# An attention backward kernel on Trainium2: where the fp32 transposes of the result tile stand, and which blocks of the exponentials TensorE transposes beside them

## The chip, the cores and the metric

One core of a Trainium2 chip. The metric is the device time of one execution in microseconds; lower is better. Before: 2212.41 us, the median of three runs (2210.66 to 2218.44). A step of the loop below takes about 1.6 us, so most times in this text are in nanoseconds.

## The reference

The kernel computes a transformer block and all its gradients in one launch: x of 2048 x 512, 32 heads of 16, an MLP of width 1792. Cut to what matters:

```python
def _A_ref(x, wqkv, wo):                       # attention
    qkv = (x @ wqkv).reshape(B, S, 3, H, Dh).transpose(2, 0, 3, 1, 4)
    q, k, v = qkv[0], qkv[1], qkv[2]
    scores = jnp.einsum("bhqd,bhkd->bhqk", q, k) * (Dh ** -0.5)
    p = softmax(scores, axis=-1)
    o = jnp.einsum("bhqk,bhkd->bhqd", p, v)
    return o.transpose(0, 2, 1, 3).reshape(B, S, D) @ wo
...
x = A_x
xn = _layernorm(x)
s = _A_ref(xn, A_wqkv, A_wo)
g = _silu(_B_ref(xn, B_w1, B_b1, B_w2, B_b2))  # the MLP
return x + s * g
...
_out, _vjp = jax.vjp(_f, A_x, A_wqkv, A_wo, B_w1, B_b1, B_w2, B_b2)
_grads = _vjp(grad_out)
```

The change lies in the attention part alone, where the forward pass and the backward pass of q, k and v are done together.

## The kernel before

`attention_core` works through 64 *blocks*: 16 pairs of heads, times four chunks of 512 queries. A block has 16 *steps*, one for each 128 keys, so there are 1024 steps, counted by `g`; `g % 16` is the place in the block. Per step and for both heads of the pair these quantities are made, with the names that the profile uses:

- `s` (L1093): scores of 128 keys by 512 queries for each head, two matmuls into one PSUM tile of two banks; there is one such tile.
- `ets` (L1102): ScalarE's exp of `s`, 128 x 1024, written into a ring in SBUF that holds 12 steps. This is E, in eight blocks of 128 keys by 128 queries (two heads, four query blocks).
- `d` (L1115): dO times V, two matmuls, each into a PSUM bank of its own out of a pool of three (`ps_d`).
- `gts` (L1132): VectorE's product of `d` and `ets`, two multiplies of 128 x 512.
- `tT` (L1177): seven of the eight blocks of E, transposed by TensorE into one PSUM tile (`ps_t`, one buffer); the eighth goes through a DMA (`ekd`). ScalarE and VectorE copy `tT` into the SBUF tiles `ek` (both L1189): `VCOPY` says for each place in the block how many of the seven VectorE takes, ScalarE takes the rest. Where VectorE takes some, ScalarE's copy waits for VectorE's.
- `X` (L1207, L1210, L1214): sums over the 16 steps of a block, in one PSUM bank, 128 x 512 fp32: the numerators of o and dq, the row sums, and others, all with queries along the free dimension.
- `Z` (L1291): dK and dV of an earlier block, from the transposed E (`ek`) and the DMA-transposed `gts` (`gk`), weighted by `W`; four matmuls a step, 20 steps behind. VectorE adds Z to `acc` (L1303, L1305) at places 3 and 11.

The order on each engine is the order of the code (no scheduler moves anything). The loop for step `g` emits:

```python
emit_d(g, 0); emit_s(g + 1, 0); emit_s(g + 1, 1); emit_d(g, 1)
emit_exp(g + 1)
emit_T(g - 1)
emit_XT(g)
emit_x(g - 1, "e"); emit_x(g - 1, "l"); emit_x(g - 1, "g")
emit_z(g + ZOFF)
emit_mult(g)
emit_xs(g - 1)
emit_fin(g)
...
emit_acc(g + ZOFF)
...
emit_cT(g - 1, 0, 7 - VCOPY[(g - 1) % 16], nc.scalar.copy)
emit_dmat(g)
```

So TensorE runs d, s, s, d, the transposes of the step before, (XT), X, Z. ScalarE runs the exp of the next step and then the copy of the last step's `tT`. VectorE runs the first multiply, its share of the `tT` copy (inside `emit_mult`), the second multiply, and at some places one copy or addition more.

After the last step of a block, VectorE copies X to SBUF (`xs`, L1223, at place 0 of the next block). At place 2 (`FIN_AT`) TensorE transposes `xs` in four fp32 pieces of 128 x 128 (`XT`, L1233) into a tile that takes a turn in the pool of `d`; VectorE copies it (`xt`, L1245, 512 columns) and takes the reciprocal of the row sums (`rL`, L1255); GpSimd makes from it the weights `W` that Z needs from place 4 on, and the parts of o and dq (L1256 to L1271). Four GpSimd lines of these need the second half of XT (XG) only.

The DMA transposes of `gts` and of the eighth block of E (L1148, L1158, L1162, L1164) stand in SyncE's queue and read the ring of E and `gts`.

Of the kernel before, what the change touches and what calls it, by code (L numbers as in the profile page):

```python
# [8 lines left out]
bf16 = mybir.dt.bfloat16  # L9
f32 = mybir.dt.float32  # L10
ACT = mybir.ActivationFunctionType
ALU = mybir.AluOpType
# [1016 lines left out]
def attention_core(ctx, ctx_r, tc, k, grads, Oall, dQall, dKVT_out, ident_f32, ident_bf, npairs=16, nqc=4):  # L1029
    nc = tc.nc  # L1030
# [3 lines left out]
    ps_t = ctx.enter_context(tc.tile_pool(name="ps_t", bufs=1, space=PSUM, reuse_waits="tile"))  # L1034
    ps_d = ctx.enter_context(tc.tile_pool(name="ps_d", bufs=3, space=PSUM, reuse_waits="tile"))
# [8 lines left out]
    xsp = sb("xsp", 1)  # L1044
    finp = sb("finp", 1)
# [19 lines left out]
    NB = len(blocks)  # L1065
    NSTEP = NB * 16
    st_s, st_d, st_et, st_gt, st_T = {}, {}, {}, {}, {}
    blk = [dict(Gk={}, Ek={}) for _ in range(NB)]
    cur = {}

    def a_unit(g):
        return (g // 16, g % 16) if 0 <= g < NSTEP else None
# [43 lines left out]
                         start=True, stop=True, tile_position=(r, 0))  # L1116


    VCOPY = (0, 0, 0, 0, 1, 1, 1, 2, 1, 2, 0, 0, 1, 1, 1, 0)

    def emit_mult(g):
        a = a_unit(g)
        if a is None:
            emit_cT(g - 1, 7 - VCOPY[(g - 1) % 16], 7, nc.vector.tensor_copy)
            return
        kb = a[1]
        if kb % 2 == 0:
            cur["gts"] = gtp.tile([128, 2, 2, 512], bf16, name="gts")
        gts = cur["gts"]
        st_gt[g] = gts  # L1130
        for hj in range(2):
            nc.vector.tensor_tensor(out=gts[:, kb % 2, hj, :].rearrange("k (b q) -> k b q", b=4),  # L1132
                                    in0=st_d.pop((g, hj))[:].rearrange("k (b q) -> k b q", b=4),
                                    in1=st_et[g][:, :, hj, kb % 4, :], op=ALU.mult)
            if hj == 0:
                emit_cT(g - 1, 7 - VCOPY[(g - 1) % 16], 7, nc.vector.tensor_copy)

    def emit_dmat(g):
# [12 lines left out]
        sl = g // 4 % 3  # L1151
        if kb % 8 == 4:
            ek = ekd.tile([128, 2, 4, 128], bf16, name="ekd")
            blk[j]["Ek"][(kc - 1, 3)] = ek[:, 0]
            blk[j]["Ek"][(kc, 3)] = ek[:, 1]
            blk[j]["ekd"] = ek
            if sl == 0:
                nc.sync.dma_start_transpose(out=ek[:, 0], in_=ets[:, 2, 3, 1].rearrange("k a q -> k (a q)"))  # L1158
        if kb % 8 == 6:
            ek = blk[j].pop("ekd")  # L1160
            if sl == 0:
                nc.sync.dma_start_transpose(out=ek[:, 1], in_=ets[:, sl, 0, 0].rearrange("k a q -> k (a q)"))  # L1162
            else:
                nc.sync.dma_start_transpose(out=ek[:].rearrange("q c a k -> q (c a) k"),  # L1164
                                            in_=ets[:].rearrange("k s b h a q -> k (s b h) (a q)")[:, 8 * sl - 1:8 * sl + 1]
                                            .rearrange("k x q -> k (x q)"))

    def emit_T(g):
        a = a_unit(g)
        if a is None:  # L1170
            return
        kk = a[1] % 4
        et = st_et[g]
        t = ps_t.tile([128, 7, 128], bf16, name="tT")
        for i in range(7):
            b = i + a[1] // 4 % 2
            nc.tensor.transpose(t[:, i, :], et[:, b // 2, b % 2, kk, :], ident_bf[:])  # L1177
        st_T[g] = t
        if kk == 0:
            cur["ek"] = ekc.tile([128, 4, 7, 128], bf16, name="ek")  # L1180
            blk[a[0]]["Ek"][a[1] // 4] = cur["ek"]

    def emit_cT(g, lo, hi, copy):

        a = a_unit(g)
        if a is None or lo == hi:
            return
        j, kb = a
        copy(out=blk[j]["Ek"][kb // 4][:, kb % 4, lo:hi].rearrange("q i k -> q (i k)").bitcast(f32),  # L1189
             in_=st_T[g][:, lo:hi].rearrange("q i k -> q (i k)").bitcast(f32))  # L1190

    def emit_x(g, part):
        a = a_unit(g)
# [23 lines left out]
    def emit_xs(g):  # L1217
# [5 lines left out]
        nc.vector.tensor_copy(out=xs[:], in_=blk[j].pop("X")[:])  # L1223
        blk[j]["xs"] = xs

    def emit_XT(g):
        j = g // 16 - 1
        if g % 16 != FIN_AT or not 0 <= j < NB:
            return
        xs = blk[j].pop("xs")  # L1230
        XT = ps_d.tile([128, 4, 128], f32, name="XT", tag="d")
        for qb in range(4):
            nc.tensor.transpose(XT[:, qb, :], xs[:, qb * 128:(qb + 1) * 128], ident_f32[:])  # L1233
        blk[j]["XT"] = XT

    def emit_fin(g):
        j = g // 16 - 1
        if g % 16 != FIN_AT or not 0 <= j < NB:
            return
        p, qc = blocks[j]  # L1240
        NQq = k.op0["NATQq"]
        NQd = k.op0["NATQd"]
        XT = blk[j].pop("XT")
# [10 lines left out]
        rL = finp.tile([128, 4, 2, 1], f32, name="rL")  # L1254
        nc.vector.reciprocal(out=rL[:], in_=XG[:, :, :, 17:18])  # L1255
        nc.gpsimd.tensor_tensor(out=W2[:, :, :, 16:32], in0=nqs, in1=bc(rL[:]), op=ALU.mult)  # L1256
        ndl = finp.tile([128, 4, 2, 1], f32, name="ndl")
        nc.gpsimd.tensor_tensor(out=ndl[:], in0=XG[:, :, :, 0:1], in1=rL[:], op=ALU.mult)
        ndr = finp.tile([128, 4, 2, 1], f32, name="ndr")
        nc.gpsimd.tensor_tensor(out=ndr[:], in0=ndl[:], in1=rL[:], op=ALU.mult)  # L1260
        nc.gpsimd.tensor_tensor(out=W1[:, :, :, 0:16], in0=ndo, in1=bc(rL[:]), op=ALU.mult)
        nc.gpsimd.tensor_tensor(out=W1[:, :, :, 16:32], in0=nqs, in1=bc(ndr[:]), op=ALU.mult)
# [8 lines left out]
        nc.gpsimd.tensor_tensor(out=dQv, in0=t1[:], in1=bc(rL4[:]), op=ALU.mult)  # L1271

    def emit_z(g):
        u = z_unit(g)
# [39 lines left out]
    FIN_AT = 2  # L1314
# [5 lines left out]
    for g in range(NSTEP - ZOFF):  # L1320
        cur["g"] = g
        a = a_unit(g)
        if a is not None:
            j, kb = a
# [12 lines left out]
        emit_d(g, 1)  # L1337
# [3 lines that stand above are left out]
        emit_x(g - 1, "e")  # L1341
        emit_x(g - 1, "l")
        emit_x(g - 1, "g")
# [4 lines that stand above are left out]
        for it in [x for x in late if x[0] <= g]:  # L1348
            late.remove(it)
# [127 lines left out]
```

## Time and profile before

The profiled execution took 2212.67 us, of which 2210.8 us are the span from its first to its last instruction. The attention loop fills the span from 221.7 to 1867.4 us.

| What | Instructions | Busy, us | Mean of one, ns |
|---|---|---|---|
| multiply `gts`, VectorE L1132 | 2048 | 1361.6 | 683 |
| exp `ets`, ScalarE L1102 | 1024 | 1047.7 | 1023 |
| transposes `tT`, TensorE L1177 | 7168 | 568.1 | 219 |
| copy of `tT`, ScalarE L1189 | 1024 | 502.2 | 490 |
| matmuls `d`, TensorE L1115 | 2048 | 459.1 | 385 |
| matmuls `s`, TensorE L1093 | 2048 | 401.3 | 380 |
| copy of `tT`, VectorE L1189 | 576 | 131.6 | 229 |
| addition of Z to `acc`, VectorE L1305 | 96 | 65.5 | 682 |
| copy of XT, VectorE L1245 | 64 | 43.5 | 680 |
| fp32 transposes `XT`, TensorE L1233 | 256 | 38.9 | 274 |

Busy time is the union of the instructions' spans; since instructions of one engine overlap at their ends, the mean of one times their count is more than the busy time for matmuls that run side by side. The granted clock of TensorE was 0.997 of full speed over the whole span. The chain of waits lists the work that ended last, followed back from the end; its largest lines are `tT` (24% of the span), `d` (15%), `X` L1207 (10%), `Z` (10%).

### The profile page before, as it was taken

To read this page: it belongs to the slowest core of one execution; us is meant where nothing else is said; L and a number is where in the kernel's file an instruction comes from. 1 tells how busy PE (TensorE), PEld (TensorE's weight loads), DVE (VectorE), ACT (ScalarE), POOL (GpSimd) and SP (SyncE) were. 2 spreads that over 40 slices of the span, in tenths; PEclk is the share of its full clock that TensorE was granted. 3 is DMA by queue.
4 is the path that set the end of the run, shared out by engine and by line. 5 is a ranking of instruction groups with operands and counts; after the bars stand their busy time and mean duration, and the time that the engine had idled before them with its cause. 6 is when DMAs were issued, how large, how long until landed. Compare 5 with 4: busy or idle time off the path is not lost.

```text
span 2210.8 us, 74213 instructions
## 1 busy us (share of the span) xinstructions
PE 2154.0 (97%) x30690; PEld 1203.2 (54%) x30690; DVE 1911.7 (86%) x3638; ACT 1734.2 (78%) x2481; POOL 590.4 (27%) x1373
## 2 busy tenths in 40 slices
PE   6999999999999999999999999999999999999998
PEld 3444555555555555555555555555555555444444
DVE  6677899999999999999999999999999998797624
ACT  4664888888888888888888888888888887784214
POOL 4375213221222222221322122222222132510002
PEclk9999999999999999999999999999999999999999
DMA  7786999999999999999999999999999999999974
GB/s 232 244 277 200 200 199 192 202 198 194 204 205 195 204 196 197 201 197 202 200 196 203 199 195 198 206 194 204 197 197 206 197 210 211 300 259 235 244 200 156
DMA packets 1422066, 461.14 MB, mean 209 GB/s; under 512 B 1334622, under 2 KB 1405918, under 8 KB 1421728
## 3 DMA queue, kind: packets, MB, share of 16 engines
q1 hardware_dynamic: 1407424, 425.46, 101.4%
q0 software_dynamic: 12720, 29.37, 5.0%
q8 instruction: 240, 3.93, 0.8%
q10 hardware_dynamic: 1584, 1.57, 0.2%
q14 instruction: 98, 0.80, 0.1%
HBM read 62.79 MB, written 64.75 MB: 58 GB/s over the span
## 4 chain that ended last, share of the span: by engine, by line
PE 89%; DVE 4%; ACT 2%; issue 2%; DMA 2%; POOL 1%; SPq 1%; ACTq 0%; DVEq 0%; POOLq 0%
PE tT L1177 24%; PE d L1115 15%; PE X L1207 10%; PE Z L1291 10%; PE X L1210 5%; PE X L1214 5%; PE s L1093 3%; PE ps_dw L742 2%; PE ps_dy L912 2%; PE ps_h L352 2%; PE ps_dw L984 2%; PE ps_m L367 2%; PE ps_dh L878 2%; PE XT L1233 1%; PE ps_qkv L210 1%
## 5 line engine op out<-in xcount | busy, mean ns | idle before, releaser
L1132 DVE TENSOR_TENSOR gts<-d,ets 128x512 bf16<-128x512 f32 x2048 | 1361.6, 683 | 99.4 <-ACT ek L1189 20.5
L1102 ACT ACTIVATE ets<-s 128x1024 bf16<-128x1024 f32 x1024 | 1047.7, 1023 | 198.6 <-PE s L1093 95.5
L1177 PE MATMUL tT<-ident_bf,ets 128*128 128x128 bf16 x7168 | 568.1, 219 | 11.7 <-ACT ek L1189 1.7
L1177 PEld LDWEIGHTS <-ets 128*128 128x128 bf16 x7168 | 444.6, 97 | 237.6 <-issue 235.5
L1189 ACT COPY ek<-tT 128x448 f32<-128x448 f32 (+2 forms) x1024 | 502.2, 490 | 2.8 <-DVE ek L1189 2.1
L1115 PE MATMUL d<-QDT,KVT 32*128 32x512 bf16 x2048 | 459.1, 385 | 0.0
L1093 PE MATMUL s<-QDT,KVT 32*128 32x512 bf16 x2048 | 401.3, 380 | 3.7 <-ACT ets L1102 3.6
L1115 PEld LDWEIGHTS <-KVT 32*128 32x128 bf16 x2048 | 145.6, 91 | 323.3 <-issue 323.3
L1207 PE MATMUL X<-ets,NAT 128*32 128x256 bf16 x4096 | 300.4, 284 | 0.3 <-DVE xs L1223 0.3
L1210 PE MATMUL X<-ets,Lc 128*32 128x256 bf16 x4096 | 289.5, 273 | 0.0
L1214 PE MATMUL X<-gts,NAT 128*17 128x256 bf16 x4096 | 289.5, 273 | 0.0
L1351 POOL COPY tick<-gts 1x2 bf16<-1x2 bf16 x205 | 35.7, 174 | 612.3 <-DVE gts L1132 612.3
L1291 PE MATMUL Z<-gk,W 128*32 128x512 bf16 x2048 | 197.9, 379 | 1.0 <-DVE acc L1305 1.0
L1291 PE MATMUL Z<-ek,W 128*32 128x512 bf16 x1792 | 198.4, 379 | 0.0
L1207 PEld LDWEIGHTS <-NAT 128*32 128x32 bf16 x4096 | 106.0, 93 | 110.8 <-issue 11.3
L1256 POOL TENSOR_TENSOR W<-NATQq,rL 128x128 bf16<-128x128 bf16 x64 | 25.4, 396 | 526.1 <-DVE rL L1255 438.4
L1093 PEld LDWEIGHTS <-KVT 32*128 32x128 bf16 x2048 | 139.2, 91 | 12.8 <-issue 9.6
L1189 DVE COPY ek<-tT 128x64 f32<-128x64 f32 (+1 forms) x576 | 131.6, 229 | 0.7
L1291 PEld LDWEIGHTS <-W 128*32 128x32 bf16 x4096 | 109.8, 97 | 11.5 <-issue 1.5
L1210 PEld LDWEIGHTS <-Lc 128*32 128x32 bf16 x4096 | 107.8, 96 | 0.0
L1214 PEld LDWEIGHTS <-NAT 128*17 128x17 bf16 x4096 | 103.4, 92 | 3.0
L1291 PE MATMUL Z<-ekd,W 128*32 128x512 bf16 x256 | 97.0, 379 | 0.0
(246 smaller groups left out, 2318.7 us busy)
## 6 DMA issues: line engine op xcount, KB each, us to landing
gk<-gts SPq DMA_TRANSPOSE x512, 5.3
H1T_s<-h1r SPq DMA_DIRECT2D x28, 256.0 KB, 4.1
HGT_s<-hgT SPq DMA_DIRECT2D x8, 896.0 KB, 4.5
DH_s<-stg SPq DMA_DIRECT2D x12, 512.0 KB, 3.2
hch<-DH_s SPq DMA_DIRECT2D x12, 512.0 KB, 4.4
gp<-H1T_s SPq DMA_DIRECT2D x9, 512.0 KB, 7.6
out_dram<-ob_w POOLq DMA_DIRECT2D x36, 128.0 KB, 4.2
NAT_s<-NS SPq DMA_DIRECT2D x4, 1056.0 KB, 6.1
```

Of the source, the lines that this page charges most:

```text
L352: nc.tensor.matmul(ps[:], lhsT=w1_sb[:, ic, fc * 128:(fc + 1) * 128], rhs=yT[:, ic, g * 512:(g + 1) * 512], start=(ic == 0), stop=(ic == I ...
L367: nc.tensor.matmul(ps[:], lhsT=hgT[:, g % 2, fc, t4 * 128:(t4 + 1) * 128], rhs=w2_sb[:, fc, :], start=(fc == 0), stop=(fc == FC - 1))
L1093: nc.tensor.matmul(s[:, hj, :], lhsT=op["KVT"][r:r + 32, kb * 128:(kb + 1) * 128], rhs=op["QDT"][r:r + 32, qc * 512:(qc + 1) * 512], start ...
L1102: nc.scalar.activation(out=st_et[g][:, :, :, a[1] % 4, :].rearrange("k b h q -> k h b q"), in_=cur["s"][:].rearrange("k h (b q) -> k h b q ...
L1115: nc.tensor.matmul(d[:], lhsT=op["KVT"][r:r + 32, kb * 128:(kb + 1) * 128], rhs=op["QDT"][r:r + 32, qc * 512:(qc + 1) * 512], start=True, ...
L1132: nc.vector.tensor_tensor(out=gts[:, kb % 2, hj, :].rearrange("k (b q) -> k b q", b=4), in0=st_d.pop((g, hj))[:].rearrange("k (b q) -> k b ...
L1177: nc.tensor.transpose(t[:, i, :], et[:, b // 2, b % 2, kk, :], ident_bf[:])
L1189: copy(out=blk[j]["Ek"][kb // 4][:, kb % 4, lo:hi].rearrange("q i k -> q (i k)").bitcast(f32), in_=st_T[g][:, lo:hi].rearrange("q i k -> q ...
L1207: nc.tensor.matmul(X[r:r + 32, 0:256], lhsT=NATt[:, kb, hj, 1:33], rhs=ev, start=(kb == 0), stop=False, skip_group_check=True, tile_positi ...
L1210: nc.tensor.matmul(X[r:r + 32, 256:512], lhsT=Lc[:], rhs=ev, start=False, stop=False, skip_group_check=True, tile_position=(0, r))
L1214: nc.tensor.matmul(X[r:r + 17, 256:512], lhsT=NATt[:, kb, hj, 0:17], rhs=gv, start=False, stop=(kb == 15), skip_group_check=True, tile_pos ...
L1291: nc.tensor.matmul(Z[r:r + 32, :], lhsT=WT[j % 2][1 - part][:, qb, hj, :], rhs=mv, start=(part == 0 and qb == 0), stop=(part == 1 and qb = ...
```

## The change

XT is made in two halves, in the steps at places 2 and 3 (`fin_half`): first the half with the row sums (half 1), then the other. Each half is two fp32 transposes, written into the upper half of the PSUM tile that the same step's `tT` uses (the tile is now a full bank of 512 fp32 columns). To make room, the `tT` of places 1 and 2 leave out their first three blocks (`cut`), six in all. These six are transposed one each in the `tT` of places 4 to 9 as an eighth block (`older`), and copied by VectorE (`emit_cO`) into the `ek` tile that they belong to. VectorE copies each half of XT back over `xs` (`emit_xt`, 256 columns) between its two multiplies. GpSimd's chain is split in two accordingly: W2, ndl, ndr and W1 with half 1, Oall, t1, rL4 and dQall with the other. `VCOPY` becomes 0 at places 4 to 9, so ScalarE copies all seven blocks there, four at places 1 and 2. The first block of the loop is left as it was.

```diff
-    VCOPY = (0, 0, 0, 0, 1, 1, 1, 2, 1, 2, 0, 0, 1, 1, 1, 0)
+    VCOPY = (0, 0, 0, 0, 0, 0, 0, 0, 0, 0, 0, 0, 1, 1, 1, 0)
...
             if hj == 0:
                 emit_cT(g - 1, 7 - VCOPY[(g - 1) % 16], 7, nc.vector.tensor_copy)
+                emit_cO(g - 1)
+                emit_xt(g)
+
+    def emit_cO(g):
+        if a_unit(g) is None or not older(g):
+            return
+        kk, i = older(g)
+        nc.vector.tensor_copy(out=blk[g // 16]["Ek"][0][:, kk, i].bitcast(f32), in_=st_T[g][:, 448:512])
...
+    def cut(g):
+        return 3 if g >= 16 and g % 16 in (1, 2) else 0
+
+    def older(g):
+        n = g % 16 - 4
+        return (1 + n // 3, n % 3) if 16 <= g < NSTEP and 0 <= n < 6 else None
...
-        t = ps_t.tile([128, 7, 128], bf16, name="tT")
-        for i in range(7):
+        t = ps_t.tile([128, 512], f32, name="tT")
+        tb = t[:].bitcast(bf16).rearrange("q (i k) -> q i k", k=128)
+        for i in range(cut(g), 7):
             b = i + a[1] // 4 % 2
-            nc.tensor.transpose(t[:, i, :], et[:, b // 2, b % 2, kk, :], ident_bf[:])
+            nc.tensor.transpose(tb[:, i - cut(g), :], et[:, b // 2, b % 2, kk, :], ident_bf[:])
+        if older(g):
+            kk2, b = older(g)
+            nc.tensor.transpose(tb[:, 7, :], st_et[g // 16 * 16 + kk2][:, b // 2, b % 2, kk2, :], ident_bf[:])
...
+    def fin_half(g):
+        j = g // 16 - 1
+        if not 0 <= j < NB or g % 16 not in (FIN_AT, FIN_AT + 1):
+            return None
+        return j, (1, 0)[g % 16 - FIN_AT]
+
     def emit_XT(g):
...
-        XT = ps_d.tile([128, 4, 128], f32, name="XT", tag="d")
-        for qb in range(4):
-            nc.tensor.transpose(XT[:, qb, :], xs[:, qb * 128:(qb + 1) * 128], ident_f32[:])
-        blk[j]["XT"] = XT
+        t = st_T[g - 1] if a_unit(g - 1) is not None else ps_d.tile([128, 512], f32, name="XT", tag="d")
+        XT = t[:, 256:512].rearrange("q (b c) -> q b c", b=2)
+        for b in range(2):
+            qb = 2 * h + b
+            nc.tensor.transpose(XT[:, b, :], xs[:, qb * 128:(qb + 1) * 128], ident_f32[:])
+        blk[j]["XT"] = t[:, 256:512]
+
+    def emit_xt(g):
...
+        j, h = f
+        nc.vector.tensor_copy(out=blk[j]["xs"][:, 256 * h:256 * h + 256], in_=blk[j].pop("XT"))
...
     def emit_fin(g):
...
-        xt = xsp.tile([128, 4, 128], f32, name="xt", tag="xs")
-        nc.vector.tensor_copy(out=xt[:], in_=XT[:])
-        xf = xt[:].rearrange("q b c -> q (b c)")
+        xf = blk[j]["xs"][:]
...
+        if half == 1:
+            rL = finp.tile([128, 4, 2, 1], f32, name="rL")
+            nc.vector.reciprocal(out=rL[:], in_=XG[:, :, :, 17:18])
...
+            blk[j]["r"] = rL, ndl
+            return
+        rL, ndl = blk[j].pop("r")
...
```

More of the change, by code (lines that the diff above doesn't have):

```diff
@@ L1188, in emit_cT @@
         j, kb = a
+        c = cut(g)
+        lo = max(lo, c)
         copy(out=blk[j]["Ek"][kb // 4][:, kb % 4, lo:hi].rearrange("q i k -> q (i k)").bitcast(f32),
-             in_=st_T[g][:, lo:hi].rearrange("q i k -> q (i k)").bitcast(f32))
+             in_=st_T[g][:, (lo - c) * 64:(hi - c) * 64])
     def emit_x(g, part):
@@ L1253, in emit_fin @@
         bc = lambda ap: ap.to_broadcast([128, 4, 2, 16])
[L1254 to L1262, printed above, removed]
+        if half == 1:
+            rL = finp.tile([128, 4, 2, 1], f32, name="rL")
+            nc.vector.reciprocal(out=rL[:], in_=XG[:, :, :, 17:18])
+            nc.gpsimd.tensor_tensor(out=W2[:, :, :, 16:32], in0=nqs, in1=bc(rL[:]), op=ALU.mult)
+            ndl = finp.tile([128, 4, 2, 1], f32, name="ndl")
+            nc.gpsimd.tensor_tensor(out=ndl[:], in0=XG[:, :, :, 0:1], in1=rL[:], op=ALU.mult)
+            ndr = finp.tile([128, 4, 2, 1], f32, name="ndr")
+            nc.gpsimd.tensor_tensor(out=ndr[:], in0=ndl[:], in1=rL[:], op=ALU.mult)
+            nc.gpsimd.tensor_tensor(out=W1[:, :, :, 0:16], in0=ndo, in1=bc(rL[:]), op=ALU.mult)
+            nc.gpsimd.tensor_tensor(out=W1[:, :, :, 16:32], in0=nqs, in1=bc(ndr[:]), op=ALU.mult)
+            blk[j]["r"] = rL, ndl
+            return
+        rL, ndl = blk[j].pop("r")
         Ov = Oall[:, st0:st0 + 4, p * 32:(p + 1) * 32].rearrange("q b (h c) -> q b h c", h=2)
@@ L1271, in emit_fin @@
         nc.gpsimd.tensor_tensor(out=dQv, in0=t1[:], in1=bc(rL4[:]), op=ALU.mult)
+        blk[j].pop("xs")
     def emit_z(g):
```

16 lines of the change are left out of this document (10 added, 6 removed).

## The prediction

> **What bounds the kernel now.** I read the page first. TensorE is the chain:
>
> ```profile
> PE 2154.0 (97%) x30690; PEld 1203.2 (54%) x30690; DVE 1911.7 (86%) x3638; ACT 1734.2 (78%) x2481; POOL 590.4 (27%) x1373
> ...
> PE 89%; DVE 4%; ACT 2%; issue 2%; DMA 2%; POOL 1%; SPq 1%; ACTq 0%; DVEq 0%; POOLq 0%
> ...
> L1189 ACT COPY ek<-tT 128x448 f32<-128x448 f32 (+2 forms) x1024 | 502.2, 490 | 2.8 <-DVE ek L1189 2.1 <-PE tT L1177 0.6
> ```
>
> But matmul ends are modelled, so 97% does not say that no more fits in. For that I cut the attention stretch (221.7 to 1867.4 us, 64 blocks of 16 steps) at the starts of ScalarE's exp (L1102). Slot n runs from the exp of step n (in its block) to that of step n+1. The stretch view of one undisturbed block, slots 0 to 6:
>
> ```profile
> 659.45:661.01 1.56, 1.56 (x30) 0.90 (x29) 1.37 (x3) 1.39 (x2) 0.06 (x1) 1.00 1.29 240
> 661.01:662.57 1.56, 1.53 (x29) 0.89 (x28) 1.51 (x3) 1.45 (x2) 0.62 (x2) 1.00 1.15 258
> 662.57:664.19 1.62, 1.60 (x30) 0.97 (x30) 1.62 (x4) 1.45 (x3) 0.00 (x0) 1.00 1.33 132
> 664.19:666.17 1.98, 1.98 (x35) 1.25 (x34) 1.95 (x4) 1.45 (x3) 0.00 (x0) 1.00 1.02 228
> 666.17:667.73 1.56, 1.53 (x29) 0.88 (x27) 1.56 (x4) 1.45 (x3) 1.25 (x5) 1.00 1.25 286
> 667.73:669.33 1.60, 1.57 (x29) 0.94 (x29) 1.53 (x4) 1.45 (x2) 1.52 (x5) 1.00 0.56 127
> 669.33:670.89 1.56, 1.56 (x30) 0.90 (x29) 1.39 (x3) 1.39 (x2) 1.18 (x4) 1.00 1.28 293
> ```
>
> Columns: length, then busy time of PE, PEld, DVE, ACT, POOL, the clock, DMA. A slot is 1.56 us; only slot 3 is 1.98. The timeline says why, and what sets 1.56:
>
> ```profile
> 661.01 1.02 ACT L1102 ACTIVATE ets<-s 128x1024 bf16<-128x1024 f32 x1 [0.17 <-PE d L1115]
> 661.93 0.53 ACT L1189 COPY ek<-tT 128x448 f32<-128x448 f32 x1
> 662.03 0.38 PE L1115 MATMUL d<-QDT,KVT 32*128 32x512 bf16 x1
> 662.09 0.39 PE L1093 MATMUL s<-QDT,KVT 32*128 32x512 bf16 x2
> 662.51 0.55 PE L1177 MATMUL tT<-ident_bf,ets 128*128 128x128 bf16 x7
> ...
> 664.07 0.55 PE L1177 MATMUL tT<-ident_bf,ets 128*128 128x128 bf16 x7
> 664.46 0.61 PE L1233 MATMUL XT<-ident_f,xs 128*128 128x128 f32 x4
> 665.00 0.29 PE L1207 MATMUL X<-ets,NAT 128*32 128x256 bf16 x4
> ...
> 667.35 0.68 DVE L1305 TENSOR_TENSOR acc<-Z,acc 128x512 f32<-128x512 f32 x1
> 667.95 2.04 DVE L1132 TENSOR_TENSOR gts<-d,ets 128x512 bf16<-128x512 f32 x3
> ```
>
> From the same records, as medians over the blocks, in ns (E is the slot's exp start):
> - exp takes 1023; s, which overwrites what exp reads, starts at E+1075 or 3 after the first d, whichever is later. From s to the next exp is 487 when d went out 35 or more earlier, 520 when s comes right behind d (slots 2, 5, 13: 1613, 1600, 1601). 1075+487 = 1562 is the slot: a ring of TensorE and ScalarE, in which the first d arrives at about E+1023, some 50 early.
> - second d to first tT 362; tT to X 480 with seven transposes, 55.5 for each more or fewer; X to the next first d 660.
> - ScalarE's copy of tT (one buffer) starts at E+920 and takes 527, 473, 420 for 7, 6, 5 blocks, so 366 for 4 (estimate, 54 a block); the next tT starts 52 after it. After a copy of seven that is E+1499, 50 later than TensorE could.
> - VectorE, start to start: multiply 598, a copy of 512 columns 598, of 128 198, of 64 131, the reciprocal 121; a multiply lasts 679, and the d that reuses its buffer starts 53 after it.
> - four XT put 55+116+110+109+202 = 592 between the last tT and X, in place of 147: +445, slot 3's excess.
>
> The sixteen slots of a block without a late DMA sum to 25,523.
>
> **Part by part.** *XT out of one step, in two pairs.* Steps 2 and 3 issue four tT and two XT: 3x55.5+55+116+202 = 540 from tT to X, against 480. First d of slot 3: 1499+540+660 past the exp of slot 2 (1613 long), at 1086, so the slot is 1089+520 = 1609, not 1981: -372. Slot 4: d at 1049, s on time, 1565: +3. Slot 5: d at about 1030, 1564, -36, because ScalarE copies four blocks only in slots 3 and 4. The new wait there, tT (and ScalarE's copy, which waits too) on VectorE's copy of XT, ends at about E+1020, so ScalarE ends near 1420 and tT starts at 1470 at the latest, a few ns late. Behind acc, which slips with VectorE to 635 of slot 5, waits Z of step 4, due at 727: no loss, by 40 after the hand-over.
>
> *The copy of XT: two of 256 columns for one of 512.* No row has that width; the ends are 198 and 598 each. I take 331, since 131, 198 and 598 lie on a line of 1.04 ns a column. VectorE's work then moves: it does multiply, xt, multiply, reciprocal in step 2 (1648), and multiply, xt, multiply, acc in step 3 (2125), against slots of 1609 and 1565. Its first multiply of step 4 starts about 560 into slot 5, ends at 1240, and the second d of step 5, which takes the buffer that this multiply frees (three in turn, two a step), starts at 1295 in place of 1084. The cover that xt and acc had before is gone: slot 3's extra 372, in which VectorE caught up. Behind this d on TensorE stand step 5's transposes; with eight of them (below) the next d comes at 1295+362+536+660-1564 = 1289 of slot 6, which is then 1292+520 = 1812, not 1564: +248. Were the copies 198 wide in time there would be no late d and slot 6 would be 1656 (-156 on my sum); at 598 it would grow by 534.
>
> *The six left-out blocks, one in each of steps 4 to 9.* 55.5 each on TensorE, which the 50 of slack would nearly hide, had ScalarE's copy stayed at 384 or 320 columns. VCOPY is set to 0 there, so ScalarE copies all seven: tT starts at E+1499. 1499+536+660-1562 = 1133: s comes right behind d, and the slot is 1136+520 = 1656; from there the next tT starts at 1505, d at 1045, and that slot is 1562. So 1562 and 1656 alternate in slots 7 to 11, against 1562: +93, +94 and +10 (slot 11 was 1552). Slots 12 to 14 alternate too, seven transposes behind full copies: 1600, 1562, 1600 against 1562, 1601, 1562: +37. Slot 15 takes 1562 for 1552: +10.
>
> *VectorE's other copies*: 9 per block before, 7 of 64 and 2 of 128 columns, 9 of 64 after: -134 of work off the path in slots 6 to 14, worth nothing while TensorE waits for ScalarE. GpSimd's chain starts after the same reciprocal, some 0.4 us earlier; Z needs W two steps on. No DMA moves in its queue.
>
> Sum: -372+3-36+248+93+94+10+37+10 = +87 ns; with roundings of some 10 per slot, +75. In 63 blocks: +4.7 us. The profiled execution spans 2210.8 of 2212.67 us, and the median of the three runs is 2212.41; so span 2215.5, **2217 us**. The late-d penalty of 33 (520 less 487) is taken from rows; the Trainium skill ("TensorE: Matmul & The Clock Gate", The cost: per-tile semaphore tail) has completions of concurrent tiles queue for their semaphores at 26.3 ns each. Four more late slots at 7 less would make the sum 2 us smaller; three slots of this trace say 33.
>
> **The rivals.** *1: it all fits, faster.* Only slot 3's loss shows: -372 x 63 = -23.4, **2189 us**. For it: the added 55.5 is hardly more than the 50 of slack. Against: rows 1, 2, 4 and 12 of the medians all show the tT held to E+1499 by a full copy, and the d late in the next slot. Half of it (no late d in step 5, the rest as forecast) gives 2207.
>
> *2: ScalarE queues behind VectorE, slower.* The built program has ScalarE's copy wait for VectorE's copy out of the same tile wherever there is one: now steps 1, 2 (xt), 4 to 9 (the older block) and 12 to 14. In the trace it then starts 34 after VectorE's end. VectorE's copy of 211 must start by E+675 or ScalarE slips from E+920; in slots where VectorE's first multiply started at E+66 the copy began at 673, on the edge; in slot 12's successor the multiply started at E+207. At 130 late in each of the six slots, the two-slot ring (3218) grows by 130: 6 x 65 = 390 a block, +24.6: **2242 us**; at 60 late, 2228. Against it: the forecast has these multiplies at E-30, the copies at 570. The Trainium skill ("PSUM — Partial Sum Buffer", PSUM bank collisions raise a hardware error) says any two engines must be kept off one bank, reads included; by that rule this wait can't be avoided in one 2 KB tile, and the trace agrees (0.15 us of idle ScalarE behind VectorE at 1003.98).
>
> **Chances.** Forecast (2207 to 2223 by itself) 0.52; rival 1 0.15; rival 2 0.23; the rest 0.10, of which faster 0.02, same 0.03, slower 0.05. About 0.5% (11 us) is what a measurement here can tell: faster 0.17, same 0.55, slower 0.28. Range 2200 to 2236: of rival 1 it leaves out the part near its full gain (0.09), of rival 2 the worse part (0.09), and the far end of the copy's price (2250 at 598), since three rows lie on its line.
>
> **What would show it.** Slot 3 at 1.61; slot 6 at 1.8 with the second d waiting for a multiply; slots 8 and 10 at 1.65, 7 and 9 at 1.56; XT still 256 records. Wrong: slot 6 under 1.66 (VectorE kept up), slots 7 to 10 all 1.56 (rival 1), or ScalarE's copies at more than E+920 behind VectorE in slots 7 to 11 (rival 2).

## The result and the profile after

In the first comparison the changed kernel took 2207.37 us (median of 11 runs, 2204.76 to 2211.12) against 2212.41 (median of 11, 2207.5 to 2218.44): a ratio of 0.9976 [0.9966, 0.9986], 5 us less. Three later comparisons of the same two kernels gave less: 0.9990 [0.9976, 1.0005], 0.9985 [0.9974, 0.9997] and 0.9993 [0.9981, 1.0004]. The forecast was 2217, that is 4.7 us more. So the time lies in the forecast range, and the difference is under the 0.5% that the prediction called the limit of a measurement, but it goes the other way than forecast. Most of what follows is about how an expected loss per block, which the trace shows smaller than forecast, does not appear in the time.

The page of the profiled run after (2206.27 us, span 2204.4, granted clock 0.998), in the lines that answer to those of before:

```profile
PE 2147.6 (97%) x30690; PEld 1192.5 (54%) x30690; DVE 1899.9 (86%) x3696; ACT 1758.4 (80%) x2481; POOL 590.3 (27%) x1373
...
PE 90%; DVE 4%; issue 2%; ACT 2%; DMA 2%; POOL 1%; SPq 0%; DVEq 0%; ACTq 0%; POOLq 0%
...
L1211 ACT COPY ek<-tT 128x448 f32<-128x448 f32 (+2 forms) x1024 | 510.4, 498 | 4.0 <-DVE ek L1211 1.3
```

TensorE has as many instructions as before, and the chain is still its own. VectorE has 58 more instructions (128 half copies of XT for 64 whole ones, less six copies of tT) and ScalarE's copies are 8.2 us longer in sum. Nothing here says where the change acts. The stretch view of an undisturbed block does; slots 3 to 8, with the columns as before (length, then PE, PEld, DVE, ACT, POOL, clock, DMA):

```profile
660.08:661.68 1.60, 1.60 (x30) 0.88 (x29) 1.60 (x4) 1.38 (x3) 0.00 (x0) 1.00 0.84 95
661.68:663.24 1.56, 1.56 (x28) 0.83 (x26) 1.56 (x5) 1.39 (x3) 1.26 (x5) 1.00 1.28 288
663.24:664.80 1.56, 1.56 (x27) 0.81 (x25) 1.56 (x4) 1.45 (x2) 1.48 (x5) 1.00 1.28 290
664.80:666.56 1.76, 1.76 (x32) 1.08 (x32) 1.59 (x4) 1.56 (x3) 1.38 (x4) 1.00 1.29 178
666.56:668.13 1.57, 1.53 (x30) 0.90 (x29) 1.45 (x4) 1.45 (x2) 0.89 (x3) 1.00 1.71 227
668.13:669.78 1.65, 1.65 (x31) 0.99 (x31) 1.44 (x4) 1.45 (x2) 0.61 (x2) 1.00 0.61 151
```

The long slot 3 (1.98 before) is 1.60. What was won there is lost again further on: slot 6 is 1.76 (1.56 before) and slot 8 is 1.65. VectorE is busy for the whole of slots 3, 4 and 5. As medians over the blocks, in ns, beside the forecast:

| Slot | 3 | 4 | 5 | 6 | 7 | 8 | 9 | 10 | 11 | 12 | 13 | 14 | 15 | sum of 16 |
|---|---|---|---|---|---|---|---|---|---|---|---|---|---|---|
| before | 1982 | 1562 | 1600 | 1563 | 1562 | 1563 | 1562 | 1562 | 1552 | 1562 | 1601 | 1563 | 1563 | 25,534 |
| forecast | 1609 | 1565 | 1564 | 1812 | 1562 | 1656 | 1562 | 1656 | 1562 | 1600 | 1562 | 1600 | 1562 | +75 |
| after | 1596 | 1562 | 1563 | 1758 | 1572 | 1654 | 1565 | 1656 | 1555 | 1609 | 1562 | 1601 | 1562 | 25,553 |

By the medians a block became about 20 ns longer, 1.2 us in 63 blocks. The timeline of the same block from slot 5 into slot 6 shows how slot 6 came about:

```profile
663.19 0.68 DVE L1346 TENSOR_TENSOR acc<-Z,acc 128x512 f32<-128x512 f32 x1
...
663.79 1.88 DVE L1133 TENSOR_TENSOR gts<-d,ets 128x512 bf16<-128x512 f32 x3
...
664.27 0.39 PE L1115 MATMUL d<-QDT,KVT 32*128 32x512 bf16 x1
...
664.31 0.39 PE L1093 MATMUL s<-QDT,KVT 32*128 32x512 bf16 x2
...
664.52 0.37 PE L1115 MATMUL d<-QDT,KVT 32*128 32x512 bf16 x1
...
664.82 0.56 PE L1194 MATMUL tT<-ident_bf,ets 128*128 128x128 bf16 x7
...
665.23 0.22 PE L1197 MATMUL tT<-ident_bf,ets 128*128 128x128 bf16 x1
...
666.03 0.38 PE L1115 MATMUL d<-QDT,KVT 32*128 32x512 bf16 x1
666.04 0.39 PE L1093 MATMUL s<-QDT,KVT 32*128 32x512 bf16 x2
```

VectorE, behind acc, starts the first multiply of step 4 only 0.55 into slot 5. It ends at 664.47, and the second d, which would follow s at once, goes out at 664.52: 1.28 into its slot. tT, with an eighth transpose (L1197), follows it, and the first d of slot 6 comes at 666.03, 1.23 past the exp (664.80), with s right behind. All of this is the chain of the prediction, in its order; it only runs faster than forecast between the second d and X, of which more below.

*Where the 6.4 us between the two profiled spans went.* The same records, cut at the exps, for all nine profiles of the two unchanged kernels, in us:

| Profile | ahead of the first exp | blocks 0, 1 | blocks 2 to 62 | block 63 to the end | span | exps late for the DMA of E |
|---|---|---|---|---|---|---|
| before, first | 221.7 | 51.9 | 1566.9 | 370.4 | 2210.8 | 2.3 |
| before, b2 | 218.4 | 52.0 | 1568.6 | 373.4 | 2212.4 | 3.7 |
| before, b3 | 220.4 | 50.6 | 1566.4 | 370.0 | 2207.4 | 1.8 |
| before, b4 | 218.0 | 52.9 | 1566.4 | 372.3 | 2209.7 | 2.5 |
| after, first | 218.5 | 51.8 | 1564.2 | 370.1 | 2204.4 | 0.6 |
| after, a2 | 218.5 | 51.9 | 1567.3 | 369.6 | 2207.2 | 3.6 |
| after, a3 | 219.6 | 51.8 | 1571.2 | 369.9 | 2212.7 | 6.3 |
| after, a4 | 219.7 | 51.7 | 1568.0 | 368.6 | 2208.0 | 3.7 |
| after, a5 | 222.9 | 51.7 | 1568.4 | 370.3 | 2213.4 | 3.7 |

(The last column sums, in blocks 2 to 62, the exps at places 4 and 12 that waited for the DMA transpose `ekd`, by what each came later than its median, where that is over 60 ns.) Of the 6.4 us, 3.2 lie ahead of the first exp, in code that the change does not touch and that varies from 218.0 to 222.9 over the nine profiles; 2.7 lie in the loop; 0.3 lie behind it. By the medians alone the loop would be 1.2 longer. But what single slots take beyond their medians sums to 9.3 before and 5.4 after; late DMA transposes of E (2.3 and 0.6) are under half of that difference, and the repeats of the changed kernel have more of them. Over all profiles the loop takes 1567.1 before (mean of four) and 1567.8 after (mean of five).

### The profile page after: what moved, and what is told of

It is laid out like the page before. It is cut to its first block, busy times and chain, and to the rows that moved or that the text cites. A ratio compares the mean times of both kernels' runs of the same rounds, so it can differ in the third digit from the quotient of the medians.

```text
span 2204.4 us, 74272 instructions
## 1 busy us (share of the span) xinstructions
PE 2147.6 (97%) x30690; PEld 1192.5 (54%) x30690; DVE 1899.9 (86%) x3696; ACT 1758.4 (80%) x2481; POOL 590.3 (27%) x1373
## 4 chain that ended last, share of the span: by engine, by line
PE 90%; DVE 4%; issue 2%; ACT 2%; DMA 2%; POOL 1%; SPq 0%; DVEq 0%; ACTq 0%; POOLq 0%
PE tT L1194 24%; PE d L1115 15%; PE X L1229 10%; PE Z L1332 10%; PE X L1232 5%; PE X L1236 5%; PE ps_dw L742 2%; PE ps_dy L912 2%; PE ps_dw L984 2%; PE ps_h L352 2%; PE s L1093 2%; PE ps_m L367 2%; PE ps_dh L878 2%; PE tT L1264 1%; PE ps_dwkv L830 1%
## 5 line engine op out<-in xcount | busy, mean ns | idle before, releaser
L1194 PEld LDWEIGHTS <-ets 128*128 128x128 bf16 x6790 | 429.4, 97 | 248.3 <-issue 245.6
L1194 PE MATMUL tT<-ident_bf,ets 128*128 128x128 bf16 x6790 | 545.9, 219 | 14.2 <-ACT ek L1211 2.1
L1211 ACT COPY ek<-tT 128x448 f32<-128x448 f32 (+2 forms) x1024 | 510.4, 498 | 4.0 <-DVE ek L1211 1.3
L1115 PE MATMUL d<-QDT,KVT 32*128 32x512 bf16 x2048 | 450.0, 385 | 0.0
L1115 PEld LDWEIGHTS <-KVT 32*128 32x128 bf16 x2048 | 130.1, 91 | 319.2 <-issue 319.2
L1093 PEld LDWEIGHTS <-KVT 32*128 32x128 bf16 x2048 | 123.6, 91 | 8.5 <-issue 6.1
L1197 PE MATMUL tT<-ident_bf,ets 128*128 128x128 bf16 x378 | 82.8, 219 | 0.0
```

The source lines that it names most:

```text
L1093: nc.tensor.matmul(s[:, hj, :], lhsT=op["KVT"][r:r + 32, kb * 128:(kb + 1) * 128], rhs=op["QDT"][r:r + 32, qc * 512:(qc + 1) * 512], start ...
L1115: nc.tensor.matmul(d[:], lhsT=op["KVT"][r:r + 32, kb * 128:(kb + 1) * 128], rhs=op["QDT"][r:r + 32, qc * 512:(qc + 1) * 512], start=True, ...
L1194: nc.tensor.transpose(tb[:, i - cut(g), :], et[:, b // 2, b % 2, kk, :], ident_bf[:])
L1197: nc.tensor.transpose(tb[:, 7, :], st_et[g // 16 * 16 + kk2][:, b // 2, b % 2, kk2, :], ident_bf[:])
```

## The experiments

**Both kernels once more (b2, a2).** No edit; one run each, to see which parts of the difference come again.

> The kernel before, unchanged, once more, for its profile. Slots are cut at the starts of exp as in the prediction. Theory A (the gain lies in late DMAs that got rarer: a block without one is 20 ns longer after the change, 25,553 against 25,534 as the sum of the slots' medians, but the mean over blocks 2 to 62 is 43 ns shorter): the slots' medians come back within 5 ns each, and the waits of the exp of step 12 behind late DMA transposes, 3.2 us in the first profile, come back at 2 to 5 us. Theory B (chance, or what lies outside the attention loop): those waits vary freely between profiles of one kernel, and the part before the loop, 221.7 us, varies by some 3 us too.

> The changed kernel, unchanged, once more, for its profile. Theory A: the waits of the exp of step 12 stay under 1 us (0.5 in the first profile), and the loop is again 2 to 4 us shorter than before's. Theory B: they come out anywhere between 0 and 4 us, and the stretch before the loop, 218.5 us in the first profile, moves by some 3 us.

Measured: 2214.26 and 2209.08 us. The sixteen medians came again within 2 ns (sums 25,532 and 25,555). The late exps did not: 3.7 and 3.6 us in place of 2.3 and 0.6, and the part ahead of the loop took 218.4 in b2, where the first profile of before had 221.7. The slots belong to the kernels; those other differences do not.

**Is it acc that makes the second d late? (a_noacc)** At place 3 Z goes to acc in one block of four only (the one in which it is copied); the additions of the other three at that place are left out.

```diff
-        else:
+        elif kp == 0:
             # ... the addition of Z to acc
```

> The changed kernel without VectorE's addition to acc at place 3 in three blocks of four (this part of dK and dV is left out). Theory 1 (slot 6 is 1758 long because VectorE is late after xt and acc, and the second d of step 5 waits for a multiply): in those blocks the second d of slot 5 goes out at 1084 and slot 6 falls to 1656, so the loop gains 48 x 102 = 4.9 us. Theory 2 (slot 6 is long because ScalarE's copy of tT comes 107 late behind VectorE's, at 1027): slot 6 stays above 1.7 us.

Measured: slot 6 is 1658. The timeline of slot 5 (its exp starts at 664.75) of a block without the addition:

```profile
664.11 2.00 DVE L1133 TENSOR_TENSOR gts<-d,ets 128x512 bf16<-128x512 f32 x3
...
665.78 0.39 PE L1115 MATMUL d<-QDT,KVT 32*128 32x512 bf16 x1
665.82 0.39 PE L1093 MATMUL s<-QDT,KVT 32*128 32x512 bf16 x2
665.83 0.39 PE L1115 MATMUL d<-QDT,KVT 32*128 32x512 bf16 x1
```

VectorE goes from the last multiply of step 3 straight to those of step 4. The second d goes out right behind s, 1.08 into its slot, and slot 6 falls to the 1656 that the prediction gave for no late d. That shows the wait: VectorE behind acc, with the two copies of xt ahead of it. The medians' sum fell by 102 ns, 6.2 us in 61 blocks; the loop of this one run took 1563.1, which is 4.7 less than the mean of after's five and 1.0 less than the shortest of them. The time was 2209.15.

**Is it the full copy that makes slots 8 and 10 long? (a_vcopy1, a_copy6, a_no8)** First, VectorE takes one block of seven again at places 4 to 9, beside the older block:

```diff
-    VCOPY = (0, 0, 0, 0, 0, 0, 0, 0, 0, 0, 0, 0, 1, 1, 1, 0)
+    VCOPY = (0, 0, 0, 0, 1, 1, 1, 1, 1, 1, 0, 0, 1, 1, 1, 0)
```

> The changed kernel with VCOPY 1 at places 4 to 9: ScalarE copies six blocks there, VectorE the seventh and the older one. Theory 1 (slots 8 and 10 are 1654 to 1656 long because a full copy holds tT to 1499, and the eighth transpose then makes the next d late): the copy is 54 shorter; VectorE's two copies end near 910, ScalarE starts some 25 late, tT at 1470; slots 7 to 11 alternate between 1562 and 1626, some 60 to 90 ns a block less, 4 to 6 us in all. Theory 2 (the eighth transpose alone makes them long): slots 8 and 10 stay within 10 ns of 1655. Rival 2 of the prediction (ScalarE queues behind VectorE): ScalarE's copies start 100 or more late, slots 7 to 11 grow.

Measured: 2225.8 us, 1.0046 [1.003, 1.0063] (before 2216.82 in that comparison). I had expected a gain; it is the one variant that is clearly slower. Slots 7 to 11 are 1706, 1653, 1619, 1630, 1622. The timeline of slot 6, whose exp starts at 592.03:

```profile
592.81 0.21 DVE L1211 COPY ek<-tT 128x64 f32<-128x64 f32 x1
...
592.94 0.21 DVE L1145 COPY ek<-tT 128x64 f32<-128x64 f32 x1
...
593.24 0.48 ACT L1211 COPY ek<-tT 128x384 f32<-128x384 f32 x1 [0.19 <-DVE ek L1145]
```

ScalarE's exp ends at 593.05, and its copy then waits 0.19 for VectorE's second copy out of the same tile: it starts 1.21 past the exp, in the next slots at 1.11, 1.02, 1.00, 1.01 and 1.00, where the changed kernel has 1.03 in slot 6 and 0.92 from slot 7 on. The 50 ns that ScalarE saves on a block are less than it loses by coming behind VectorE. This is the second rival's mechanism; in the changed kernel itself, with one copy of VectorE's, that copy stands at 0.56 to 0.58 in slots 8 to 11 and at 0.67 in slot 7, out of ScalarE's way. Only in slot 6, where VectorE is late, it stands at 0.78; ScalarE's copy comes behind it at 1.03, and slot 7 is 10 ns longer. The rule that the prediction cited from the Trainium skill ("PSUM — Partial Sum Buffer", PSUM bank collisions raise a hardware error) says that two engines have to keep off one bank; the trace agrees, and shows the price, which the rule does not give: these copies start 0.08 to 0.19 us later than the changed kernel's.

So I took the two parts apart without a second copy of VectorE's. In a_copy6 ScalarE copies six blocks of seven at places 4 to 9 and nobody the seventh; in a_no8 the older blocks are neither transposed nor copied. What is left out is filled with zeros by GpSimd.

```diff
# a_copy6, in emit_cT
+        if g >= 16 and 4 <= kb < 10:
+            hi = min(hi, 6)
# a_no8, in older
-        return (1 + n // 3, n % 3) if 16 <= g < NSTEP and 0 <= n < 6 else None
+        return None
```

> The changed kernel with ScalarE copying six of the seven blocks at places 4 to 9, and nobody the seventh (GpSimd writes zeros in its place; this part of dK is left out); the eighth transpose and VectorE's copy of it stay. Theory 1: tT starts at 1446 in place of 1499, slots 8 and 10 fall to 1603, slot 12 to 1562. Theory 2 (the eighth transpose alone makes the slots long): slots 8 and 10 stay at 1655. Theory 3 (the full copy alone): 7 to 11 at 1562.

> The changed kernel without the six older blocks (neither transposed nor copied; GpSimd writes zeros in their place, so this part of dK is left out). Theory 1 (slots 8, 10 and 12 are long because a full ScalarE copy holds tT to 1499 and the eighth transpose adds 56 behind it, each worth about half): slots 8 and 10 fall from 1655 to 1600, 7, 9 and 11 stay at 1562 or less. Theory 2 (the eighth transpose alone): all of 7 to 11 at 1562.

Measured: with the shorter copy slot 10 is 1604 and slot 12 1562, as expected; slot 8 stays at 1665, since the copy ahead of it starts at 0.98. Without the eighth transposes slots 8 and 10 are 1601 and slots 7 and 9 1562; the stretch view of a_no8 for slots 8 and 10:

```profile
667.00:668.61 1.61, 1.58 (x29) 0.95 (x29) 1.26 (x3) 1.45 (x3) 0.48 (x2) 1.00 0.91 201
...
670.17:671.77 1.60, 1.57 (x29) 0.94 (x29) 1.30 (x3) 1.45 (x3) 0.17 (x1) 1.00 0.74 11
```

ScalarE is as busy as in the changed kernel (1.45, a full copy), TensorE does one transpose less, and of the 91 and 94 that slots 8 and 10 had gained, 53 and 55 are gone; with the shorter copy 52 of slot 10's are. So taking out either part alone wins back a little over half, as the prediction's sum has it (1600 or 1603 in place of 1656); for slot 8 the shorter copy did not show it.

The times are the surprise: 2209.64 for a_copy6 and 2213.66 for a_no8 (one run each, before 2213.05). The medians of a_no8 sum to 25,373, 180 less than after (slot 6 is 107 shorter and slots 8 and 10 as said, but slot 4 is 50 longer, which was not looked into). That is 11.0 us in 61 blocks; yet its loop took 1572.1, 4.3 more than after's mean. ScalarE's timeline shows one of the places where it went:

```profile
1805.31 1.02 ACT L1102 ACTIVATE ets<-s 128x1024 bf16<-128x1024 f32 x1 [0.15 <-PE d L1115]
...
1810.68 1.02 ACT L1102 ACTIVATE ets<-s 128x1024 bf16<-128x1024 f32 x1 [3.92 <-DMA ekd<-ets]
```

From one exp to the next it takes 5.37 us, since the exp has to write into a part of E's ring that a DMA transpose still reads. Such late exps at places 4 and 12 sum to 14.3 us here, against 0.6 to 6.3 in after's profiles.

**Without the DMA transposes of E (a_noekd, b_noekd, a_no8_noekd).** The eighth block of E is not transposed; GpSimd fills its place with zeros. In a_no8_noekd the edit of a_no8 is made as well.

```diff
-            if sl == 0:
-                nc.sync.dma_start_transpose(out=ek[:, 0], in_=ets[:, 2, 3, 1].rearrange("k a q -> k (a q)"))
...
+            nc.gpsimd.memset(ek[:], 0.0)
```

> The changed kernel without the DMA transposes of the eighth block of E; GpSimd sets that tile to zero instead (the eighth block is left out of dK and dV). No DMA reads the ring of E any more, so no exp can wait for one. Theory A (the change is faster because fewer exps wait for late DMA transposes; block by block its steps are no shorter): this kernel and the kernel before without the same transposes come out alike, the changed one 0 to 2 us slower in the loop (19 ns more in 63 blocks). Theory C (the change shortens something else): the changed one stays some 5 us ahead.

> The kernel before without the DMA transposes of the eighth block of E, GpSimd's zeros in its place (left out of dK and dV). Theory A: the waits of exp at places 12 and 4 (4 to 5 us in two profiles) are gone, the blocks' mean falls from 25.68-25.71 to within 60 ns of the sum of the medians, 25.53, and the loop is some 4 to 7 us shorter than with them. Theory C: the difference to the changed kernel without them stays at 5 us.

> The changed kernel without the six older blocks and without the DMA transposes of the eighth block of E (zeros from GpSimd for both; left out of dK and dV). Without the older blocks alone the slots' medians summed to 25,373 but the mean block was 25,772, with 14.3 us of exps that waited for these transposes. Theory D (the ring of DMA transposes takes back what shorter slots give): with them gone the mean block falls to within 110 ns of the medians' sum, to about 25,480, and the loop over blocks 2 to 62 is 17 us shorter than 1572.1, near 1554. Theory E (the zeros that GpSimd writes held the loop): the mean block stays above 25,650.

Measured: 2207.8 us for the changed kernel without them, 0.9971 [0.9958, 0.9984], and 2209.88 for the kernel before without them, 0.9979 [0.9967, 0.9991], both against the full kernel before (2213.69). With this DMA gone the two differ by 2 us, and their intervals overlap. Their slots now sum to 25,554 and 25,562, and their loops take 1564.5 and 1565.4 us: 0.9 apart, where the slots say 0.5. The waits for `ekd` are gone from both.

a_no8_noekd took 2195.22 us (one run, before 2214.06), and its loop 1553.4. Against a_noekd its slots sum to 168 less, 10.2 us in 61 blocks, and the loop is 11.1 shorter. The same edit that gained nothing with the DMA transposes in place gains all that its slots say without them; 18.7 us lie between the loops of a_no8 and a_no8_noekd. The line of the DMA queue that holds the transposes, from the changed kernel's list of queues (packets, MB, and the packets' time as a share of 16 engines' span):

```profile
q1 hardware_dynamic: 1407424, 425.46, 101.6%
```

The same line of a_no8_noekd:

```profile
q1 hardware_dynamic: 1270880, 391.88, 90.3%
```

There are 10% fewer packets, and the DMA transposes of `gts`, which stay, land 4.4 us after issue in place of 5.3 (medians). The share passes 100%, so it does not tell how full the queue is; that a full queue makes the transposes late is not shown. What the two kernels show, with one run of each, is a second bound beside the first: in the faster slots of a_no8 the exp waits for the DMA transposes of E.

**The order of s and d (a_sfirst, b_sfirst, a_sel, b_sel).** A slot whose s comes right behind d pays 33 ns (520 in place of 487). If s went first there, the 33 should be a gain in each such slot. In the first two kernels s goes first in every step, in the others only at the places where d is late (2, 3, 6, 8, 10, 12, 14 in the changed kernel, 2, 3, 5, 13 in the one before).

```diff
-        emit_d(g, 0)
+        late_s = g % 16 in (2, 3, 6, 8, 10, 12, 14)
+        if not late_s:
+            emit_d(g, 0)
         emit_s(g + 1, 0); emit_s(g + 1, 1)
+        if late_s:
+            emit_d(g, 0)
         emit_d(g, 1)
```

> The changed kernel with both s matmuls issued ahead of both d matmuls. Theory 1 (a slot whose s comes right behind d is 33 longer, 520 against 487 from s to exp, because the completion of d is told first): the seven late slots (2, 3, 6, 8, 10, 12, 14) lose some 30 each, 230 a block, 14 us in all, if late DMAs do not take it back; d goes out 55 later in the other slots, VectorE's multiplies with it. Theory 2 (the 33 are the price of four matmuls side by side, whichever is first): the slots stay as they are, or grow because VectorE gets d later.

> The kernel before with both s matmuls issued ahead of both d matmuls. Theory 1: the three late slots (2, 5, 13) and slot 3 lose some 30 each, 100 to 130 a block, 6 to 8 us in all. Theory 2: no gain.

> The changed kernel with s ahead of d only in the seven steps in which s comes right behind d (2, 3, 6, 8, 10, 12, 14). Theory 1 (the 33 between 487 and 520 are the price of d's completion being told ahead of that of s): each of these slots falls by 30 to 40, the others stay (in the run with s first everywhere they grew, because d went out 55 later), 230 ns a block, 14 us in the loop, so some 2193 us. Rival (the loop is held by DMA transposes as well, which use the time that a shorter block leaves): the slots' medians fall as said, but late DMAs, some 2 to 5 us of the loop in every profile so far, grow and take back half or more.

> The kernel before with s ahead of d only in its late steps (2, 3, 5, 13). Theory 1: 33 off each, 130 ns a block, 8 us, some 2205 us, with the same DMA waits as before. Rival: half or more is taken back by late DMAs.

Measured: 2215.38 (1.0003 [0.9988, 1.0019]), 2211.8 (0.9995 [0.9984, 1.0007]), 2217.89 (1.0013 [0.9999, 1.0028]) and 2211.23 (0.9988 [0.9972, 1.0004]): no gain that can be told, where 14, 6 to 8, 14 and 8 us were expected at best. In the changed kernel the medians' sum even grew, to 25,593 and 25,615, since other slots grew by more than the late ones lost (in a_sel slot 4 went from 1562 to 1649; why was not looked into). In the kernel before it fell, to 25,509 and 25,498. The stretch view of b_sel for slots 5 and 6, which were 1600 and 1563, shows where most of the 130 ns expected there went:

```profile
1205.89:1207.46 1.57, 1.54 (x29) 0.91 (x29) 1.57 (x3) 1.45 (x3) 1.49 (x5) 1.00 0.73 164
1207.46:1209.06 1.60, 1.60 (x30) 0.94 (x30) 1.43 (x4) 1.40 (x3) 0.62 (x3) 1.00 1.25 284
```

The 34 ns left slot 5 and stand in slot 6; slots 13 and 14 do the same (1566, 1597). TensorE arrives in slot 6 when the copies and transposes let it, and an earlier exp does not move that. Only the 34 of slot 2 (1613 to 1579) stay won, with slot 3 as long as before (1981): 2.1 us in 61 blocks, too little to tell from the time. The Trainium skill ("TensorE: Matmul & The Clock Gate", The cost: per-tile semaphore tail) gives 26.3 ns for each completion that queues; the slot shows 33 to 34 here, and no run shows whether it is that.

**How sure is the first comparison? (a3, b3, a4, b4, a5)** Unchanged kernels again, timed; b3 and b4 are the kernel before, compared with itself.

> The changed kernel unchanged, in five rounds beside the kernel before. Theory A (block by block nothing is gained: 19 ns more by the medians; the 5 us are chance of DMA waits inside and outside the loop): 0 to 3 us faster than before, interval touching 1. Theory C (something systematic that the medians of the slots do not show): again 4 to 6 us faster, and the profile's loop again 2 us shorter, with the stretch before and after it shorter too.

> The kernel before, unchanged, as a control in five rounds against itself: ratio 1 within 0.001. Its profile gives a third value of the loop (1566.9 and 1568.6 us for blocks 2 to 62 so far) and of what lies outside it (592.1 and 591.8 with the ends; 588.6 and 588.1 for the changed kernel).

> The changed kernel unchanged, five rounds more, to settle whether the first comparison's 5 us are the change's. Theory A (no: the slots' medians are 20 ns a block longer, and late DMA transposes, 4.2 to 11.4 us of the loop in its three profiles, decide a run): 0 to 2 us from before, the interval touching 1. Theory C: 4 to 6 us faster, the interval clear of 1.

> The kernel before, unchanged, as a control beside it: ratio 1 within 0.001; the loop's late waits again 6 to 8 us.

> The changed kernel unchanged, once more in five rounds; so far 5.0, 0.9 and 3.9 us faster than before. If a small gain is the change's, 2 to 5 us faster again, with the loop over blocks 2 to 62 at 1564 to 1571 us and what lies outside it at 588 to 590 (before: 1566 to 1569 and 590 to 592). If it is chance, within 1 us.

Measured: the changed kernel 2213.0, 2209.11 and 2213.18 us, 0.9990 [0.9976, 1.0005], 0.9985 [0.9974, 0.9997] and 0.9993 [0.9981, 1.0004]; the kernel before against itself 0.9990 [0.9974, 1.0006] and 0.9997 [0.9988, 1.0006]. The four comparisons of the change have a mean of 0.9986, the two of the same kernel 0.9994. What is left for the change is 0.08%, some 2 us, less than such comparisons can tell: the four ratios lie 0.17% apart.

## Why the prediction was right or wrong, point by point

- *Slot 3, XT out of one step (-372): right.* -386. The two pairs beside four blocks of E do hide, as worked out.
- *The wait on xt in steps 2 and 3 and the price of its copy (331): right.* ScalarE's short copies start at 1.01 and 1.03 past the exp, as forecast, and nothing is late for it. From one xt's start to the multiply behind it are 0.33 us (660.64 to 660.97 in the block shown). The first multiply of step 4 starts 552 into slot 5 (560 forecast), the second d at 1283 (1295).
- *Slot 6 (+248): mechanism shown by a_noacc, size wrong.* It measured +195. The term that was mis-sized is the time from the second d to X, taken as 362+536. The 362 (to the first tT) was read from slots in which ScalarE's copy of six blocks still holds tT back: E+920, 473 long, and 52 more is E+1445, and the second d went out at E+1084. Slots 9 and 11 of the same profile, where the copy of five ends earlier, show what it takes when nothing else holds: 317 to tT and 495 from there to X, 812 in all in place of 842. The two cases stand side by side in slots 8 and 9 of the kernel before:

```profile
673.38 0.47 ACT L1189 COPY ek<-tT 128x384 f32<-128x384 f32 x1
...
673.54 0.39 PE L1115 MATMUL d<-QDT,KVT 32*128 32x512 bf16 x1
673.90 0.55 PE L1177 MATMUL tT<-ident_bf,ets 128*128 128x128 bf16 x7
...
674.94 0.42 ACT L1189 COPY ek<-tT 128x320 f32<-128x320 f32 x1
...
675.10 0.39 PE L1115 MATMUL d<-QDT,KVT 32*128 32x512 bf16 x1
675.42 0.56 PE L1177 MATMUL tT<-ident_bf,ets 128*128 128x128 bf16 x7
```

In slot 5 of the changed kernel the d is so late that the copy (its end is 140 ahead of tT) no longer holds: 304 to tT and 550 to X, 854 in place of 898. That is 44 of the 53; the start of that d, 12 early, is the rest. With 14 in slot 3, and 11 and 7 in slots 15 and 11 (below), the sum of +87 loses 85; slot 7 and slots 12 to 14 are 19 longer than forecast, and the medians give +19. The same reading bears on "50 later than TensorE could": by slots 9 and 11 tT could start at E+1401, 98 ahead of what a copy of seven allows.

- *Slots 8 and 10 (+93, +94): right*, +91 and +94, and a_copy6 and a_no8 show both halves of it. *Slots 12 to 14 (+37)*: +46; *slots 7 and 9*: +10 and +3. *Slot 11 (+10)*: +3. *Slot 15 (+10)*: -1, a misreading: the profile of before has 1563 there as the median, not 1552 (a quarter of the blocks have about that), so the sixteen slots sum to 25,534, 11 more than the 25,523 of the prediction.
- *XT still 256 records, no move of GpSimd's or SyncE's work that counts:* as forecast. None of the three signs named as fatal came: slot 6 is over 1.66, slots 7 to 10 are not all 1.56, and the copies of slots 7 to 11 start at 0.92.
- *The step that failed is the last one: "sum +87, with roundings +75; in 63 blocks +4.7 us; so span 2215.5".* Its size was wrong for the reasons above: in place of +4.7 the slots give +1.2. And it took for granted that everything beside the medians stays as in the one profile of before. Between the two first profiles that everything came to -7.6 us, more than the sum: 3.2 less ahead of the loop, 3.9 less beyond the medians in it, the rest behind it and in the first blocks. It varies as much between runs of one kernel: late DMA transposes of E from 0.6 to 6.3 us, 218.0 to 222.9 us ahead of the loop, 368.6 to 373.4 behind block 62. Why all of it together was on the fast side in the first comparison, by 5 us in the medians of 11 runs, stays open. The chance from -5 to +5 us was in the range, but not in the reasoning; the half percent that I named as the limit of a measurement was the better guide.
- *Rival 1* (all fits, 2189) did not happen: slots 6, 8, 10, 12 and 14 are long. Its half, 2207, is the time of the first comparison to the microsecond, but it stood for a kernel without the late d in step 5, and that d is late in the trace. The agreement is chance. *Rival 2* did not happen in slots 7 to 11 either, though its mechanism is real (a_vcopy1, +9 us; slot 6 of the changed kernel, at 10 ns).

So why does taking 386 ns out of each block, 24 us in all, change the time by 0.14% in the mean of four comparisons, where a kernel against itself gave 0.06%? It is given back inside the block: 195 in slot 6, because the long slot was the time in which VectorE caught up with its extra work; 185 in slots 8 and 10, because an eighth transpose and a seventh block in ScalarE's copy use up the 50 ns of slack that the ring of TensorE and ScalarE has; 46 in slots 12 to 14. And what is won back there by leaving work out does not reach the time in full while the exp also waits for the DMA transposes of E (a_no8 against a_no8_noekd).

Two things stay open. A gain of some 2 us, if it is real, does not come from the slots: after's loop is 0.7 longer by the means of all profiles. In the part behind the loop, after's profiles are 1.8 shorter in the mean (369.7 against 371.5); but the last addition to acc comes 0.1 later in it, and the spread arises in later code that the change does not touch, which in b_sel, a variant of the kernel before, was as short (369.2) as in after. With the variants counted in, the difference shrinks to 0.6 (370.9 in seven profiles of the kernel before and its variants, 370.3 in thirteen of the changed kernel and its). Whether fewer late waits there belong to the change was not tried. And no variant run here, with all of its work in it, was clearly faster than the changed kernel (b_sel, at 2211.23, is level with the 2213.0 of the same comparison).

## What to carry to other kernels

A long slot need not be only a loss: before taking it away, ask which engine uses it to catch up, and follow that engine's next dependence two or three steps on (here VectorE, xt and acc, and a d that had never been late). A median is the time of the engine that holds the step, which need not be the one whose instruction it stands at: before a "time from d to tT" goes into a sum, look for rows in which nothing else could hold it (here 317 in place of 362). A small gain in one slot has to be followed into the next, because the next slot can give it back (b_sel). And where an engine also waits for DMA, the sum of median steps tells the shape of a block and not the time: compare means with medians, and run the unchanged kernel against itself before believing a difference of 0.2%.

## What the runs showed of the hardware that was not expected

- From the second d to the first transpose behind it are 317 ns when nothing else holds the transpose (slots 9 and 11 before, d and s together), 304 behind the late d of slot 5 after. Where ScalarE's copy holds it, it starts 51 to 52 behind the copy's end, and X then follows 14 sooner (481 in place of 495 behind seven transposes).
- A faster loop can wait longer for DMA: 14.3 us of late exps in a_no8 against 3.6 in the mean of after's five profiles, with one exp 3.9 us late (one run of a_no8). Without the DMA transposes of E, with 1.27 in place of 1.41 million packets in the queue, the effect is gone.
- Every eighth block has a slot 279 ns longer than its median (slot 8 of blocks 3, 11 and so on before, slot 2 of blocks 6, 14 and so on after), in every profile of the full kernels; the exp then waits for s. It makes some 2.2 us in either kernel. Its cause was not looked into.
